# Sixteen attention heads of a fused attention and MLP kernel run ahead of the MLP, with 1024-column exponentials

## The chip, the cores and the metric

One core of a Trainium2 chip. The metric is the device time of one execution in microseconds (us), the median of the runs shown. Engines are named as in the profile: PE is TensorE, DVE is VectorE, ACT is ScalarE, POOL is GpSimd, SP is SyncE. Here POOL issues the loads from HBM, which cast fp32 to fp16; SP issues the stores, the small copies and the DMA transposes.

## What is computed

Causal attention with a forget gate, then a two-layer MLP on its output:

```python
scores = matmul(q, k.T) / sqrt(64)                  # q, k, v: (8 batches, 8 heads, 576, 64)
cum = cumsum(log(clip(f, 1e-4, 1)))                 # f: (8, 8, 576)
scores = where(causal, -1e9, scores + cum[:, None] - cum[None, :])
x = softmax(scores) @ v                             # reshaped to (4608, 512)
h = x @ w_in                                        # w_in: (512, 2048)
out = (h - tanh(h)) @ w_out                         # w_out: (2048, 512), out: (4608, 512) fp32
```

## The kernel before

Attention goes by *pairs* of heads of one batch, 32 pairs, each in one *slot*. The scores of a pair are held transposed (keys on partitions) in seven tiles (`TILES`, L264): three of 512 columns per head, and tile 3 (`LAST`) of 128 columns that holds the last key block of both heads. `scores` (L274) does one tile: matmuls over 67 rows (64 of the head and three rows that add the decay `cum`, which SP copies into `QT` and `KT`, L168 to L180) into one of two PSUM banks, then one exponential on ACT into an fp16 tile `e`. In the first four slots (`early`) the causal mask is added by a further matmul (L295), for the first pair's tiles 0 and 1 the decay also comes by matmuls (`direct`, L289); in all later slots POOL masks `e` with an affine_select (L311). `values` (L314) multiplies the exponentials with V and normalises on DVE into `xn`; `turn` (L338) brings `xn` into the ring `XR` of MLP inputs, for batch 0 by transposes on PE and a copy, later by two DMA transposes on SP.

Q and K of batches 0 and 1 are loaded by `load_qk` (L84), turned on PE by `trans` (L242) and copied into `QT` and `KT` by DVE, with every second column of the target written by one copy. Q and K of batches 2 to 7 are loaded in blocks of 128 rows (`load_block`, L89), turned by five DMA transposes each on SP (`turn_block`, L94) and put in place by four DVE copies each (`place`, L98). `LOADS` (L198, L212 to L225) says at which tile of which slot each of these is emitted. `spin` (L237) is matmuls of no use to the result.

The MLP goes by *units* of 512 tokens, nine in all. A first-layer step (`mlp1`, L369) is four matmuls of 512 columns, a tanh on ACT and an add on DVE; there are 16 per unit. The second layer of unit 0 is 16 plain steps (`mlp2`, L438); of the other units it is 14 half products (`product`, L394) of eight 256-column matmuls each, a seven-product scheme with sums of activations on DVE (`sums`, L383) and with sums of the weights (`wsum`, L233), which are made once, in slots 7 to 10. A store to the output (`settle`, L423) goes out on SP.

The order on every engine is the order of emission. Slots 0 to 4 have lists by hand (`BEGIN`, `ORDER`, `THEN`, L454 to L456); into slot 4 three MLP steps are mixed, into slots 5 to 32 seven or eight each (L520), evenly among the score tiles. What is left, 62 steps, runs at the end alone.

Of the kernel before, what the change touches and what calls it, by code (L numbers as in the profile page):

```python
# [22 lines left out]
def kernel(  # L23
# [31 lines left out]
    aex = ctx.enter_context(tc.tile_pool(name="aex", bufs=10))  # L55
# [72 lines left out]
    pick_k = WS[3].rearrange("p k e -> p (k e)")[:, 0:512]  # L128
    pick_q = cst.tile([P, P], FP16)
# [4 lines left out]
    EL = [cst.tile([P, 192], FP16, tag=f"el{i}", name=f"el{i}") for i in range(3)]  # L134
    nc.vector.memset(id16, 0.0)
# [5 lines left out]
    nc.vector.memset(minus16, -1.0)  # L141
    nc.vector.memset(neg16, 0.0)
    nc.vector.memset(tri16, 0.0)
    nc.gpsimd.affine_select(out=neg16, in_=neg16, compare_op=ALU.not_equal,
# [3 lines left out]
    for i in range(2):  # L148
        nc.vector.memset(KT[i][:, :, S:PITCH], 0.0)
    nc.vector.memset(pick_k, 0.0)  # L150
    nc.vector.memset(pick_q, 0.0)
    nc.vector.memset(cqs[NH:P, :], 0.0)
    nc.vector.tensor_scalar(out=lf, in0=lf, scalar1=0.0001, scalar2=1.0,
                            op0=ALU.max, op1=ALU.min)
    nc.scalar.activation(out=lf, in_=lf, func=AF.Ln)
    nc.vector.memset(pick_k[0:1, :], -1.0)
    nc.vector.memset(pick_q[0:1, :], 1.0)
# [5 lines left out]
    nc.scalar.activation(out=cq, in_=cum, func=AF.Copy, bias=-SHIFT * inv_qscale, scale=inv_qscale)  # L163
    nc.vector.scalar_tensor_tensor(out=clo, in0=cum, scalar=inv_qscale, in1=chi,
                                   op0=ALU.mult, op1=ALU.subtract)
    nc.vector.memset(pick_k[NH:NH + 1, :], -1.0)

    def load_aug(b):  # L168
        i, h0 = b % 2, b * H
        nc.sync.dma_start(out=KT[i][D:D + 1, :, 0:S], in_=chi[h0:h0 + H, :])  # L170
        nc.sync.dma_start(out=QT[i][D + 2:D + 3, :, :], in_=cq[h0:h0 + H, :])
        nc.sync.dma_start(out=KT[i][D + 1:D + 2, :, 0:S], in_=cc[NH + h0:NH + h0 + H, :])

    def const_rows(i):
        nc.sync.dma_start(out=QT[i][D:D + 2, :, :], in_=minus16)
        nc.sync.dma_start(out=KT[i][D + 2:D + 3, :, 0:S], in_=ones16[0:H, :])

    const_rows(0)
    load_aug(0)
    const_rows(1)  # L180
    load_qk(qn, q, 0, 4, H)
    load_qk(kn, k, 0, 4, H)
    for e in EL:
        nc.gpsimd.memset(e, 0.0)
    for i in range(2):
        nc.gpsimd.memset(vn[i][D:P, NJ - 1, :, :], 0.0)
        nc.gpsimd.memset(vn[i][:, :, :, D:VW], 1.0)
    load_v(0)
# [5 lines left out]
    def load_wout(t0, t1):  # L194
# [3 lines left out]
    LOADS = {(0, 0): [lambda: load_qk(qn, q, 1, 0, 2), lambda: load_qk(kn, k, 1, 0, 2),  # L198
                      lambda: load_win(0, DFF // 2)],
             (0, 3): [lambda: load_qk(qn, q, 1, 2, H), lambda: load_qk(kn, k, 1, 2, H)],  # L200
             (1, 0): [lambda: load_v(1)],
             (1, 3): [lambda: load_win(DFF // 2, DFF)],
             (2, 0): [lambda: load_wout(0, NFT // 2)],
             (3, 0): [lambda: load_wout(NFT // 2, NFT)]}
# [4 lines left out]
    for n in range(4):  # L209
        for i in range(2):  # L210
            LOADS.setdefault((NPAIR + 3 + n, 1 + 3 * i), []).append(lambda n=n, i=i: wsum(n, i * K2 // 2, (i + 1) * K2 // 2))
    for b in range(2, B):  # L212
        p0 = (b - 1) * NPAIR
        q0, k0, v0, tq, tk = {2: (5, 10, 21, 14, 16), 3: (-2, 3, 9, 6, 12)}.get(b, (-7, 0, 7, 4, 11))
        for n in range(NJ):
            at_tile(p0, q0 + n, lambda b=b, n=n: load_block(qb, q, b, n))
            at_tile(p0, k0 + n, lambda b=b, n=n: load_block(kb, k, b, n))
            at_tile(p0, v0 + n, (lambda b=b, n=n: load_v_block(b, n, 0, H)) if n < NJ - 1 else lambda b=b: load_v_rest(b))
            at_tile(p0, tq, lambda b=b, n=n: turn_block(TQ, qb, b, n))
            at_tile(p0, tk, lambda b=b, n=n: turn_block(TK, kb, b, n))  # L220
        at_tile(p0, 0, lambda b=b: load_aug(b))
        for n, (dst, src) in enumerate(((QT, TQ), (KT, TK))):
            for a in range(2):
                for c in (0, 2):
                    at_tile(p0 + 3, 2 * n + a + (n + 1 if b == 2 else 0), lambda b=b, dst=dst, src=src, a=a, c=c: place(dst, src, b, a, c))  # L225
# [11 lines left out]
    def spin(n):  # L237
        t32 = ps_tr.tile([P, UW], FP32, tag="tr", name="spin")
        for _ in range(n):
            nc.tensor.matmul(out=t32, lhsT=ones16[:, 0:P], rhs=ones16[:, 0:UW])  # L240

    def trans(b, c, src, dst, early, eng, by_head=False):  # L242
        pn, g3 = S // NT6, NT6 // 2
        if early:
            t32 = ps_m.tile([P, UW], FP32, tag="m", name="t32")
        else:
            t32 = ps_tr.tile([P, UW], FP32, tag="tr", name="t32")
        t16 = t32.bitcast(FP16)[:, 0:2 * S // 2].rearrange("p (a g n) -> p a g n", a=2, g=g3)
        for a in range(2):
            for g in range(g3):  # L250
                nc.tensor.transpose(out=t16[:, a, g, :],  # L251
# [315 lines left out]
```

## Time and profile before

| | us |
|---|---|
| median of 3 runs | 357.75 (355.23 to 357.9) |
| the profiled execution | 358.62 |
| its span, first to last instruction | 356.9 |
| PE / DVE / ACT / POOL busy in the span | 339.8 / 257.4 / 218.8 / 165.3 |
| mean granted PE clock | 0.974 of full |

The page's second part cuts the span into 40 slices and shows busy tenths for each engine. The chain follows the work that ended last back to the start. A group line gives the source line, engine, operation, output and input tiles with shapes, the count, then busy time and mean ns of one, then idle time of the engine before them and what ended it. A "q" behind an engine's name (SPq) is its instruction queue, where DMAs are issued.

### The profile page before, as it was taken

Reading aid. Unit: us, or ns where it says so; the run is one execution under the profiler, and the core shown is the slowest. Engines: PE = TensorE matmul, PEld = TensorE weight load, DVE = VectorE, ACT = ScalarE, POOL = GpSimd, SP = SyncE. Lnnn points to the kernel's source line nnn. Section 1 sums busy time; section 2 is a strip of 40 time slices with the busy share of each in tenths; the row PEclk is TensorE's granted clock in tenths of the full one; section 3 lists DMA queues with packets and bytes.
Section 4 is the critical chain, followed back from the end, with each engine's and each line's share of the span. In section 5 each row is a group of like instructions: output and inputs, shape, how many; then the busy total and the mean of one; then the engine's idle time right before and its main releaser. Section 6 shows DMA issues by size and latency. Waiting matters only on the chain.

```text
span 356.9 us, 8463 instructions
## 1 busy us (share of the span) xinstructions
PE 339.8 (95%) x3192; PEld 229.8 (64%) x3192; DVE 257.4 (72%) x501; ACT 218.8 (61%) x416; POOL 165.3 (46%) x324
## 2 busy tenths in 40 slices
PE   6698799999999999999999999999999999899995
PEld 3366455555567756887887568756887786386474
DVE  8557489963899489938893899389838855864871
ACT  6468377557775587558755875587558734533630
POOL 8941157498757755775567557753222310000000
PEclk9769889999999999999999999999999999999999
DMA  7999999999999997999799989994221112002002
GB/s 106 160 203 188 208 103 112 131 181 166 152 117 109 159 172 83 102 150 175 94 107 148 189 84 93 159 184 59 55 94 28 26 50 90 2 29 91 0 17 103
DMA packets 157469, 39.98 MB, mean 112 GB/s; under 512 B 142276, under 2 KB 155828, under 8 KB 157428
## 3 DMA queue, kind: packets, MB, share of 16 engines
q0 software_dynamic: 100128, 18.36, 70.3%
q1 hardware_dynamic: 57300, 21.09, 33.5%
q8 instruction: 25, 0.41, 0.5%
q14 instruction: 16, 0.13, 0.1%
HBM read 36.85 MB, written 9.44 MB: 130 GB/s over the span
## 4 chain that ended last, share of the span: by engine, by line
PE 79%; DVE 10%; ACT 3%; DMA 3%; SPq 2%; issue 2%; DVEq 0%; ACTq 0%
PE hps L366 29%; PE px L413 15%; PE ps L287 12%; PE pm L413 12%; PE av L322 8%; DVE gt L379 4%; PE ops L444 2%; DVE sm L392 2%; DMA QT<-cqs 2%; ACT e L301 2%; ACT th L373 2%; SPq L96 1%; DMA TK<-kn 1%; PE t L251 1%; DVE xn L334 1%
## 5 line engine op out<-in xcount | busy, mean ns | idle before, releaser
L366 PE MATMUL hps<-XR,win 128*128 128x512 f16 (+4 forms) x704 | 143.7, 344 | 2.0 <-DVE gt L379 2.0
L301 ACT ACTIVATE e<-ps 128x512 f16<-128x512 f32 x192 | 110.9, 596 | 30.5 <-PE ps L287 19.4
L373 ACT ACTIVATE th<-hps 128x512 f32<-128x512 f32 x144 | 86.3, 599 | 53.4 <-PE hps L366 47.1
L379 DVE TENSOR_TENSOR gt<-hps,th 128x512 f16<-128x512 f32 x144 | 96.7, 686 | 23.7 <-ACT th L373 22.1
L311 POOL TENSOR_SCALAR_AFFINE_SELECT e<-e 128x128 f16<-128x128 f16 x168 | 62.4, 373 | 107.8 <-ACT e L301 107.4
L366 PEld LDWEIGHTS <-win 128*128 128x128 f16 x704 | 62.4, 98 | 53.4 <-issue 7.2
L287 PE MATMUL ps<-QT,KT 67*128 67x64 f16 (+5 forms) x384 | 77.8, 285 | 5.1 <-DMA QT<-cqs 2.7
L287 PEld LDWEIGHTS <-KT 67*128 67x128 f16 (+1 forms) x384 | 37.5, 100 | 28.8 <-issue 6.4
L413 PEld LDWEIGHTS <-gt 128*128 128x128 f16 x512 | 48.0, 97 | 10.2 <-DVE gt L379 1.3
L413 PEld LDWEIGHTS <-sm 128*128 128x128 f16 x384 | 36.1, 97 | 5.4
L322 PEld LDWEIGHTS <-e 128*128 128x128 f16 x896 | 33.0, 98 | 5.6 <-issue 1.7
L322 PE MATMUL av<-vn,e 128*128 128x65 f16 x896 | 34.8, 195 | 1.3 <-DVE xn L334 1.0
L434 DVE TENSOR_TENSOR ost<-pm,part 128x512 f32<-128x512 f32 x24 | 16.5, 686 | 22.7 <-PE pm L413 8.2
L428 ACT ACTIVATE part<-px 128x512 f32<-128x512 f32 x24 | 14.3, 597 | 30.1 <-PE px L413 30.1
L413 PE MATMUL pm<-ws,gt 128*128 128x256 f16 x256 | 32.2, 272 | 0.0
L413 PE MATMUL px<-ws,sm 128*128 128x256 f16 x256 | 31.5, 272 | 0.0
L110 POOL DMA_DIRECT2D vn<-in_v_dram x32 | 28.4, 889 | 2.5 <-issue 1.4
L332 DVE TENSOR_SCALAR rs<-av 128x10 f32<-128x10 f32 (+1 forms) x33 | 5.3, 160 | 32.2 <-PE av L322 32.2
L334 DVE TENSOR_TENSOR xn<-av,rs 128x640 f16<-128x640 f32 (+1 forms) x33 | 26.5, 804 | 1.3 <-DMA out_dram<-ost 0.2
L91 POOL DMA_DIRECT2D qn<-in_q_dram x30 | 25.9, 864 | 2.1 <-issue 1.8
L91 POOL DMA_DIRECT2D kn<-in_k_dram x30 | 25.5, 849 | 1.4 <-issue 1.2
L413 PE MATMUL pm<-wout,gt 128*128 128x256 f16 x128 | 17.2, 273 | 0.2 <-DVE gt L379 0.2
(74 smaller groups left out, 291.9 us busy)
## 6 DMA issues: line engine op xcount, KB each, us to landing
out_dram<-ost SPq DMA_DIRECT2D x36, 256.0 KB
vn<-in_v_dram POOLq DMA_DIRECT2D x32, 128.0 KB, 6.3
qn<-in_q_dram POOLq DMA_DIRECT2D x24, 128.0 KB, 4.0
kn<-in_k_dram POOLq DMA_DIRECT2D x24, 128.0 KB, 5.1
win<-in_moe_w_in_dram POOLq DMA_DIRECT2D x2, 1024.0 KB, 11.8
wout<-in_moe_w_out_dram POOLq DMA_DIRECT2D x2, 1024.0 KB, 17.1
XR<-xn SPq DMA_TRANSPOSE x56
vn<-in_v_dram POOLq DMA_DIRECT2D x8, 64.0 KB, 6.9
```

Source lines behind the costliest of these rows:

```text
L91: nc.gpsimd.dma_start(out=dst[b % 2][0:pn, n, :].rearrange("p (h d) -> p h d", h=H), in_=src[b, :, n * P:n * P + pn, :].rearrange("h p d - ...
L110: nc.gpsimd.dma_start(out=vn[b % 2][:, n, h0:h1, 0:D], in_=v[b, h0:h1, n * P:(n + 1) * P, :].rearrange("h p d -> p h d"))
L287: nc.tensor.matmul(out=ps[:, col:col + n], lhsT=KT[b % 2][0:rows, h, j * P:(j + 1) * P], rhs=QT[b % 2][0:rows, h, i0:i0 + n], start=True, ...
L301: nc.scalar.activation(out=e[:, lo:hi], in_=ps[:, lo:hi], func=AF.Exp, scale=qscale)
L311: nc.gpsimd.affine_select(out=view, in_=view, compare_op=ALU.is_ge, fill=0.0, base=0, pattern=pat, channel_multiplier=-1)
L322: nc.tensor.matmul(out=av[:, a, ib, :], lhsT=E.pop((b, c, a, j, ib)), rhs=vn[b % 2][:, j, 2 * c + a, 0:D + 1], start=(j == 0), stop=(j == ib))
L334: nc.vector.tensor_tensor(out=xn[:, :, h0 * D:(h0 + hn) * D].rearrange("p i (a d) -> p a i d", a=hn), in0=av[:, h0:h0 + hn, :, 0:D], in1=r ...
L366: nc.tensor.matmul(out=hps[:, o:o + n], lhsT=win[:, ci, ft * P:(ft + 1) * P], rhs=XR[:, ci, t:t + n], start=(ci == 0), stop=(ci == NCH - 1))
L373: nc.scalar.activation(out=th, in_=hps, func=AF.Tanh, scale=-1.0)
L379: nc.vector.tensor_tensor(out=GT[(u, ft)], in0=hps, in1=th, op=ALU.add)
L413: nc.tensor.matmul(out=ps[:, g * E2:(g + 1) * E2], lhsT=left(k), rhs=right[:, k, :], start=(first and g == 0 and k == 0), stop=(k == K2 - ...
L434: nc.vector.tensor_tensor(out=ost, in0=ps, in1=PART.pop((u, {2: 1, 7: 5, 4: 6}[n])), op=ALU.add)
```

## The change

- Batches 0 and 1 become eight slots with hand-written lists (`FIRST`); no MLP step is mixed into slots 0 to 6, and no spin follows slot 0. Slot 7 gets 4 steps. Slot 8 has no scores: it finishes pair 7, runs 30 MLP steps, and turns and places batch 2 between them. Then slots follow with 5 (pairs 8 to 11), 6 (pair 12), and 7 or 8 steps; 60 steps are left for the end.
- Slots 1 to 6 take score tiles in twos: two PSUM banks, one exponential of 1024 columns. The groups alternate between the two score banks (`SC`) and two of the three MLP banks (`MB`), which are idle then. The `e` tiles are twice as wide, 6 instead of 10.
- The causal mask is added by matmul in all of the first eight slots.
- `load_qk` puts rows in another order on the partitions: each row of 64 numbers is now a run of its own (128 bytes in SBUF, 768 before), and the copies after `trans` write runs of 96 columns.
- The first head gets its decay by matmuls in all its tiles (`direct`); its three rows in QT and KT are zero until slot 4. Memsets are reordered, some move from POOL to DVE and behind the first scores.
- `turn` uses PE for pair 3 alone; pairs 0 to 2 go by DMA transposes.
- Loads of batch 0, 1 and the weights are issued in one row on POOL, w_in in quarters; batch 2 follows them.
- Unit 0 takes the seven-product scheme too; the weight sums are made at steps 14, 16, 19 and 21. `mlp2` is gone.

The diff, cut to its core:

```diff
-    ps_sc = ctx.enter_context(tc.tile_pool(name="ps_sc", bufs=2, space=PSUM))
-    ps_m = ctx.enter_context(tc.tile_pool(name="ps_m", bufs=3, space=PSUM))
+    SC = ps_sc.tile([P, 2, UW], FP32, tag="sc", name="sc")
+    MB = ps_m.tile([P, 3, UW], FP32, tag="m", name="mb")
...
     def load_qk(dst, src, b, h0, h1):
-            out=dst[b % 2][:, h0:h1, :, :].rearrange("p h n d -> p h (n d)"),
-            in_=src[b, h0:h1, :, :].rearrange("h (p n) d -> p h (n d)", n=NT6))
+            out=dst[b % 2][:, h0:h1, :, :].rearrange("p h n d -> p (h n) d"),
+            in_=src[b, h0:h1, :, :].rearrange("h s d -> (h s) d").rearrange("(m p) d -> p m d", p=S // NT6))
...
-                to = dst[b % 2][0:D, h0:h0 + an, e:S:2].rearrange("d a (p g) -> d a p g", g=g3)
-                of = t16[e * D:(e + 1) * D, a0:a0 + an, :, :].rearrange("d a g p -> d a p g")
+                to = dst[b % 2][0:D, h0:h0 + an, 0:S].rearrange("d a (g e p) -> d a g e p", g=g3, e=2)[:, :, :, e, :]
+                of = t16[e * D:(e + 1) * D, a0:a0 + an, :, :]
...
+    PLACE = {0: (0, 0), 1: (0, 1), 2: (1, 0), 4: (1, 1), 5: (2, 0), 6: (2, 1)}
+    GROUPS = [(0, 1), (2, 4), (5, 6), (LAST,)]
...
+        if how == "group":
+            banks = bank("g", [SC, MB[:, 0:2, :]])
...
-        nc.scalar.activation(out=e[:, lo:hi], in_=ps[:, lo:hi], func=AF.Exp, scale=qscale)
+        nc.scalar.activation(out=eb[:, :, lo:hi], in_=banks[:, 0:n2, lo:hi], func=AF.Exp, scale=qscale)
...
+    for at, n in ((NFT - 2, 0), (NFT, 2), (NFT + 3, 1), (NFT + 5, 3)):
+        mlp[at] += [(wsum, n, 0, K2 // 2), (wsum, n, K2 // 2, K2)]
...
+    FIRST = [["8", "q0", "k0", "5", "q1", "4", "s0", "s1", "k1", "p", "s2", "s4", "s5", "q2", "r", "s6", "s3"],
+             ["g0", "g1", "k1", "g2", "va", "vb", "q2", "x", "g3"],
+             ["g0", "va", "g1", "k1", "vb", "g2", "q2", "x", "g3"],
+             ["g0", "va", "g1", "k1", "vb", "g2", "q2", "x", "g3"],
+             ["c", "g0", "va", "g1", "k1", "vb", "g2", "x", "q2", "g3"],
+             ["g0", "g1", "k1", "g2", "va", "vb", "x", "g3"],
+             ["g0", "va", "g1", "q1", "vb", "x", "g2", "k1", "g3"],
+             ["b", "s0", "va", "s1", "vb", "m", "s2", "x", "m", "s3", "s4", "m", "s5", "m", "s6"],
+             ["va", "m", "vb", "m", "x"] + ["m"] * 16 + ["tq"] + ["m"] * 4 + ["tk"] + ["m"] * 4 + ["pq"] + ["m"] * 4 + ["pk"]]
...
-            take = 0 if p < NPAIR else 3 if p == NPAIR else 7 if p <= 2 * NPAIR + 1 or p % 2 == 0 else 8
+            take = 5 if p < 3 * NPAIR else 6 if p == 3 * NPAIR else 8 - p % 2
```

In the lists, a number is that many spins, `q`/`k` a `trans` of the pair so many slots on, `s` a score tile, `g` a group of two (g3 is tile 3), `va`/`vb` the values of the slot before by head, `x` its `turn`, `m` an MLP step, `b` the loads of batch 2, `tq`/`tk` its DMA transposes, `pq`/`pk` its placement, `c` the first head's rows and batch 2's decay rows, `p` and `r` memsets (and batch 1's rows).

More of the change, by code (lines that the diff above doesn't have):

```diff
@@ L312, in scores, with values @@
                                 base=0, pattern=pat, channel_multiplier=-1)
-    def values(b, c, heads=(0, 1), apart=False):
-        if 0 in heads:
+    def values(b, c, a):
+        if a == 0:
             av = ps_av.tile([P, 2, 512], FP32, tag="av", name="av")
@@ new lines, in att_items @@
+    def att_items(p):
+        items = []
+        before = pairs[p - 1]
+        for ti in range(len(TILES)):
+            if p < len(pairs):
+                items.append((lambda ti=ti: scores(*pairs[p], (ti,), "late"), True))
+            items += [(load, False) for load in LOADS.get((p, ti), ())]
+            if ti == 1 and p > 2 * NPAIR:
+                items += [(lambda a=a: values(*before, a), a == 1) for a in range(2)]
+                items.append((lambda: turn(*before), True))
+        return items
@@ L524 @@
             for emit, counts in items:
+                emit()
                 n += counts
-                if emit is None:
-                    first = n
-            whole, n = n, 0
-            for emit, counts in items:
-                if emit is not None:
-                    emit()
-                n += counts
-                while n > first and (given + 1) * (whole - first) <= (n - first) * len(mine):
-                    fn, *args = mine[given]
-                    fn(*args)
+                while given < take and (given + 1) * whole <= n * take and STEPS[0] < len(mlp):
+                    step()
@@ L536 @@
                     given += 1
-        for fn, *args in mlp[at:]:
-            fn(*args)
+        while STEPS[0] < len(mlp):
+            step()
 _INS = ['q', 'k', 'v', 'f', 'moe_w_in', 'moe_w_out']
```

393 lines of the change are left out of this document (200 added, 193 removed).

## The prediction

> **What bounds the kernel now.** I read the page first (engines, slices, chain), then stretches of the span, the chain in order of time, and the groups by shape.
>
> ```profile
> span 356.9 us, 8463 instructions
> PE 339.8 (95%) x3192; PEld 229.8 (64%) x3192; DVE 257.4 (72%) x501; ACT 218.8 (61%) x416; POOL 165.3 (46%) x324
> ...
> PEclk9769889999999999999999999999999999999999
> ...
> PE 79%; DVE 10%; ACT 3%; DMA 3%; SPq 2%; issue 2%; DVEq 0%; ACTq 0%
> ```
>
> TensorE bounds it: busy for 95% of the span and 79% of the chain. The granted clock is below nine tenths only among the first six slices of 8.9 us, and it is these that the change rebuilds. So the question is how soon a common state is reached: both kernels have emitted 60 MLP steps (3+7+7+7+7+7+7+8+7 before, 4+30+5+5+5+5+6 after) and the scores of 13 pairs at the end of slot 12. After that only the count of steps left differs, 212 before and 210 after.
>
> ```profile
> 28.20:33.15 4.95, 4.58 (x74) 3.41 (x72) 4.35 (x8) 4.11 (x9) 0.87 (x1) 1.00 1.87 182
> 27.45:30.87 3.42, 3.04 (x38) 2.04 (x36) 3.31 (x6) 2.81 (x7) 1.35 (x2) 1.00 2.28 161
> 34.28:37.70 3.42, 1.88 (x35) 1.30 (x32) 1.62 (x4) 2.25 (x5) 0.29 (x1) 1.00 1.17 207
> 37.70:41.10 3.40, 3.40 (x19) 1.60 (x16) 0.85 (x3) 1.19 (x2) 0.69 (x2) 0.50 1.24 210
> 74.50:118.40 43.90, 43.34 (x401) 27.32 (x402) 33.47 (x66) 28.87 (x57) 33.15 (x60) 1.00 1.69 142
> 297.80:313.10 15.30, 14.28 (x66) 6.28 (x65) 12.71 (x22) 8.96 (x15) 0.00 (x0) 1.00 0.09 31
> ```
>
> Columns: stretch, its length, busy time of PE, PEld, DVE, ACT, POOL, granted clock, DMA share, GB/s. An early slot (first row) lasts 4.95 us with no engine full. Slots 8 to 12 of before are the fifth row: 43.9 us, PE 99% busy, ending at 118.4. The last row is the first layer of one MLP unit with nothing beside it: sixteen steps in 15.3 us, 0.96 each. A stretch in which PE was busy 1.88 of 3.42 us was followed by one at clock 0.50; one with 3.04 of 3.42 was not.
>
> **The change, part by part**, as a sum of stages up to the end of slot 12.
>
> *Slot 0.* Before, the second pair's scores began at 18.36:
>
> ```profile
> 8.06 5.92 DMA QT<-cqs
> ...
> 18.36 0.59 PE ps L287
> ...
> 116.80 0.88 PE px L413 x8
> ```
>
> The small row copies into QT/KT took 5.92 us to land and PE stood until they had. After, fewer memsets stand before the scan (an estimate of 0.5 us), the scale copy of cum goes between head 0's copies, and head 0's third tile needs no copied rows: one score tile (about 0.9 us at half clock) leaves the far side of the stall, and four banks drop the waits on ACT there. I take 16.3 for the start of slot 1 (bounds 15 and 18.4). The stall itself stays, and with it the half clock.
>
> *Slots 1 to 6.* The prices are those of the first 47 us, by shape:
>
> ```profile
> L301 ACT ACTIVATE e<-ps 128x512 f16<-128x512 f32 x30 | 17.6, 600 | 12.5 <-PE ps L295 8.1 <-PE ps L287 3.1 <-PE ps L292 0.8
> ...
> L262 DVE COPY QT<-t 64x576 f16<-64x576 f16 x10 | 8.0, 800 | 4.7 <-PE t L251 4.5
> ...
> L301 ACT ACTIVATE el<-ps 128x128 f16<-128x128 f32 x5 | 1.4, 274 | 2.2 <-PE ps L287 2.1 <-PE ps L295 0.2
> ...
> L348 DVE COPY XR<-x 128x576 f16<-128x576 f16 x1 | 0.5, 458 | 2.6 <-PE x L346 2.6
> ```
>
> An exponential of 512 columns takes 0.600 us, of 128 columns 0.274: 0.85 ns a column, so 1024 columns take about 1.03 us; the other bound is two of today's, 1.20. I take 1.03, as both rows lie on one line. ACT per slot: 3x1.03+0.27 = 3.4 us (before 3.9, and 0.6 for XR). The Q and K copies no longer write with a stride: 0.46 (the unstrided copy of the last row, same size) to 0.80 us each, four per pair, so DVE needs between 4.35-4x0.34 = 3.0 and 4.35 us a slot (4.35 by the early slot's row). PE streams 3200 score, 1152 mask, 1950 value and 1152 transpose columns; at 8x256 columns in 0.88 us (the row at 116.80) that is 3.2 us. Three engines near 3.3 us, but banks tie them: group 2 reuses the two banks of group 0, and the next slot's group 0 waits until ACT has read group 2. By the same column rate PE comes to the end of group 2 after 0.56+0.45+0.61+0.28+0.45+0.63 = 2.98 us (scores 0, values, scores 1, transposes, values, scores 2), ACT starts some 0.2 later and takes 1.03: 4.3 us a slot. Bounds: 3.6 (ACT alone with its gaps) and 6.9 (all at half clock: 6.4 us of PE and half a wait). I take one slot at half clock and the rest at 4.3: 6x4.3+2.6 = 28.4, so slot 7 starts at 44.7. The masks of batch 1 now cost PE 4x0.49 us and POOL nothing; both are inside this. The XR transposes moved to SP: two issues of about 1.3 us a slot (the price of the SP rows below), hidden under 4.3.
>
> *Loads.* The Q and K loads of batches 0 and 1 become runs of 128 bytes instead of 768. Packets and MB in one us from 8 (768-byte rows of Q and K), in one us from 13 (128-byte rows of V), and in two us from 18 (weights):
>
> ```profile
> q0 software_dynamic: 171, 0.13, 104.6%
> ...
> q0 software_dynamic: 1151, 0.15, 251.0%
> ...
> q0 software_dynamic: 227, 0.40, 113.2%
> ```
>
> The short packets move 0.15 MB/us against 0.13, so they cost nothing here. 3.54 MB of batches 0 and 1 take 25 us from about 3, w_in 2.1 MB at 0.20 another 10.5 to 39, w_out to 49, and with seven pairs of XR transposes among them perhaps 56; step 0 needs w_in at about 46, step 16 w_out at about 63. Hidden. The Trainium skill, page "DMA: Bandwidth & Descriptors", Specifications, says that transfers below 512 B fall to read-modify-write and lose line rate. By it the change would pay on each of these loads; the two rows above show the opposite order at these sizes, so the sum leaves it out.
>
> *Slot 7* adds four MLP steps to a pair with masks on PE: 1.8+0.9+4x0.88 = 6.2 us, to 50.9.
>
> *Slot 8: MLP alone.* Two value halves and two steps 2.6 us, ten first-layer steps at 0.96, six products at 0.88: 17.5 us. VectorE also gets the weight sums, which before lay in slots 7 to 10:
>
> ```profile
> L235 DVE TENSOR_TENSOR ws<-wout x4: 682/692/760, 66.2 to 78.1; 128x1024 f16<-128x1024 f16 x4
> ```
>
> Two of them (1.4 us) stand ahead of the last first-layer add, two more ahead of the third product's operand, on an engine (DVE) that was busy 12.71 of 15.3 us in the last row above: I take 2 us (bounds 0 and 2.8). Step 21 ends at 70.4.
>
> *Batch 2's Q and K turn on SP, the decisive part.* Before, the chain ran through exactly this:
>
> ```profile
> 65.16 1.22 SPq L96
> ...
> 70.42 3.23 DMA TK<-kn
> ...
> 73.86 0.56 DVE KT L99
> ```
>
> and a store to the output takes SP's queue 0.53:
>
> ```profile
> 88.16 0.53 SPq L450 DMA_DIRECT2D out_dram<-ost  x1
> ```
>
> Five transposes in a row start 5.26 us apart, first to last: 1.31 each; the last lands 3.23 us after its start. After, SP's order is: the store of product 2 (step 21), five TQ, the store of product 7, five TK. SP starts when step 21's sum is added (0.9 us after it, an estimate: one add of 512 columns and the wait for it): 0.53+5x1.31+0.53+4x1.31+3.23+0.56 = 16.6 us, so the first score tile of batch 2 can start at 87.9. PE has twelve steps to do meanwhile (22 to 33, 10.6 us). And VectorE stands at the Q placement until TQ has landed, with the adds of steps 30 to 33 queued behind it, so that PE stops after three of them (three MLP banks) and again before the scores: some 7 us of idle PE, enough by the row at 34.28 for the clock to fall again.
>
> *Slots 8 to 12* then: 26 steps of 0.88 (22.9 us), five pairs' scores of 1.4, four pairs' values of 0.85 (each by its columns) = 33.3 us on PE; plus 0.9 for waits (before lost 0.56 of 43.9 us, and PE was ahead of POOL there), 1.7 for one 3.4 us window at half clock, and POOL:
>
> ```profile
> L311 POOL TENSOR_SCALAR_AFFINE_SELECT e<-e 128x128 f16<-128x128 f16 x168 | 62.4, 373 | 107.8 <-ACT e L301 107.4
> ...
> L91 POOL DMA_DIRECT2D kn<-in_k_dram x30 | 25.5, 849 | 1.4 <-issue 1.2
> ```
>
> Slot 8 has seven masks and seven loads on POOL, 2.6+6.1 = 8.7 us, while PE needs 6.6; the values of that pair wait for its masks: 2.4 us over two slots (0 if POOL keeps up). Sum 38.3, so slot 12 ends at 126.2 instead of 118.4: +7.8.
>
> *The rest.* Two steps fewer: unit 0 takes fourteen products of eight 256-column matmuls (0.88) instead of sixteen steps of four 512-column ones (the same 2048 columns): -1.7.
>
> **Sum**: +7.8-1.7 = +6.1 on the profiled execution's 358.62 us (span 356.9 and 1.7 around it), 364.7. That execution lies 0.9 above the median of 357.75, so I predict **363.8 us**, its own range 359 to 369.
>
> **Rivals.**
> 1. *The attention slots do not hold the clock.* The spin matmuls that filled the early slots are gone (only slot 0 has some); 3.2 of 4.3 us is 74%, between the 55% busy that lost the clock and the 89% that kept it. If every second window falls, a slot takes about 5.6: 6x1.3-2.6 = +5, 369; if it never rises, 6x2.6-2.6 = +13, 377. The Trainium skill, "TensorE: Matmul & The Clock Gate", Part 1, lets the clock fall after an idle window of about 3.4 us; no slot has such a gap, so by it 363.8 stands. The row at 34.28 is stricter: it was more than half busy.
> 2. *Not slower: the turn of batch 2 is hidden.* If K is placed when PE comes to it, 7.1 us of idle PE and 1.7 of clock go: 354.9. It decides where nine spaces between starts and the 4.85 us around them fit into the 9.7 us that PE has left, at 0.54 us per transpose, against 1.31 in the rows above; for it speaks only that the DMA queues are empty then, while the 3.23 us of landing was measured among loads. Partly so (a landing of 2 us, no POOL wait) gives 360.
> 3. *Short packets are slow.* At half the rate of Q and K's loads, 2.36 MB take 18 us more, w_out comes at about 74 instead of 63: step 16 waits some 10 us, 374. The two packet rows speak against it. (It is what the Trainium skill's "DMA: Bandwidth & Descriptors", Specifications, would lead to.)
> 4. *The wide exponential gains nothing* (1.20 us): slots of 4.5, +1: 365, not to be told from the forecast.
>
> **How the numbers follow.** Forecast with rival 4: 0.52 (0.40 slower than before by over 1%, 0.12 within 1%); rival 1: 0.15 (slower); rival 2 and its partial form: 0.27 (0.16 faster, 0.11 within); rival 3: 0.06 (slower). One per cent is about what a measurement of this kernel can tell from no change. So slower 0.61, same 0.23, faster 0.16. The range 352 to 371 leaves out the worst of rivals 1 and 3 and the best of rival 2.
>
> **What would show it.** Each step has a mark in the profile after: slot 1 starting near 16; exponentials of 1024 columns near 1.03 us; slots of 4.3 us at clock 1.00; copies into QT below 0.8 us; SP's transposes on the chain between 71 and 88, VectorE's place waiting for TQ and TK, PE idle some 7 us there; POOL ending waits in slots 8 and 9; slot 12 ending near 126. The prediction is wrong if PE is busy through 75 to 88, or if the slots run below 4 us.

## The result, and the profile after

The changed kernel takes **659.81 us** (median of 4 runs, 656.01 to 664.63) where the kernel before takes 356.56 (4 runs, 355.23 to 357.9): 1.851 times as long, 95% interval 1.834 to 1.868. Here and below a ratio compares fast runs only, which leaves out three of the seven runs of E8 (365.62 to 366.92) and one of the twelve of E12 (361.29). The forecast was 363.8 with a range to 371. It and all four rivals were wrong by hundreds of microseconds, so something is at work that none of them names.

The page of the changed kernel, its profiled execution of 664.63 us:

```profile
span 662.9 us, 8560 instructions
PE 470.7 (71%) x3266; PEld 278.6 (42%) x3266; DVE 258.2 (39%) x523; ACT 223.9 (34%) x395; POOL 161.4 (24%) x300
...
PEclk9668757756798759975976598659975965586559
```

DVE, ACT and POOL are as busy as before (258.2 against 257.4 us, 223.9 against 218.8, 161.4 against 165.3). PE has 131 us more busy time for about the same matmuls (the clock line says why: it is below full almost to the end, not in six slices) and stands idle for 662.9-470.7 = 192 us, against 17 before. What ends this idle time is in the view of waits (waiting line, what it waited for, us in total, times, longest):

```profile
ACT th L410 <- PE mb L407: 291.1, 144, 7.3
DVE gt L416 <- ACT th L410: 286.6, 140, 3.1
...
PE mb L407 <- DVE gt L416: 129.3, 105, 1.6
...
PE sc L337 <- ACT e L353: 34.7, 43, 1.0
```

The first-layer matmuls wait 105 times for the add, the add 140 times for the tanh, the tanh 144 times for the matmuls. Each waits for the other, in a ring. The kernel before had 2.0 us of waits of these matmuls for the add. The timeline, with the MLP alone (start, length, engine and instruction, in brackets the idle time before it and what ended it):

```profile
84.52 0.69 DVE L416 TENSOR_TENSOR gt<-mb,th 128x512 f16<-128x512 f32 x1 [1.67 <-ACT th L410]
85.26 1.86 PE L407 MATMUL mb<-XR,win 128*128 128x512 f16 x4 [1.41 <-DVE gt L416]
87.16 0.60 ACT L410 ACTIVATE th<-mb 128x512 f32<-128x512 f32 x1 [2.68 <-PE mb L407]
87.79 0.69 DVE L416 TENSOR_TENSOR gt<-mb,th 128x512 f16<-128x512 f32 x1 [2.58 <-ACT th L410]
88.54 1.87 PE L407 MATMUL mb<-XR,win 128*128 128x512 f16 x4 [1.41 <-DVE gt L416]
```

Four matmuls, then the tanh, then the add, then the next four matmuls: one step every 3.28 us, nothing beside anything. The same stage of the kernel before:

```profile
298.71 5.13 PE L366 MATMUL hps<-XR,win 128*128 128x512 f16 x23
298.75 0.60 ACT L373 ACTIVATE th<-hps 128x512 f32<-128x512 f32 x1 [2.07 <-PE hps L366]
299.38 0.69 DVE L379 TENSOR_TENSOR gt<-hps,th 128x512 f16<-128x512 f32 x1 [0.86 <-ACT th L373]
299.62 0.60 ACT L373 ACTIVATE th<-hps 128x512 f32<-128x512 f32 x1 [0.27 <-PE hps L366]
```

There 23 matmuls, nearly six steps, run without a gap, and the tanhs and adds of earlier steps lie beside them. The windows view of the changed kernel (length, busy PE, PEld, DVE, ACT, POOL, granted clock, DMA share, GB/s) shows what follows from the gaps:

```profile
80.00:90.00 10.00, 5.76 (x14) 1.76 (x13) 2.93 (x5) 1.79 (x3) 0.00 (x0) 0.50 0.00 0
```

The clock is at half: four matmuls take 1.86 us instead of 0.86 to 1.02.

**Theory 1 (T1).** The change makes the three MLP banks one tile, `MB [P, 3, UW]`, and the two score banks one tile, `SC [P, 2, UW]`. The waits are placed per tile, not per bank: a matmul into bank 1 of `MB` waits for the readers of bank 0. The rivals: **T2**, the clock is lost in the slots without spins and the waits only follow from it; **T3**, the order itself (eight attention slots, then the MLP alone) is what costs.

### The profile page after: what moved, and what is told of

It is laid out like the page before. It is cut to its first block, busy times and chain, and to the rows that moved or that the text cites. A ratio compares the mean times of both kernels' runs of the same rounds, so it can differ in the third digit from the quotient of the medians.

```text
span 662.9 us, 8560 instructions
## 1 busy us (share of the span) xinstructions
PE 470.7 (71%) x3266; PEld 278.6 (42%) x3266; DVE 258.2 (39%) x523; ACT 223.9 (34%) x395; POOL 161.4 (24%) x300
## 3 DMA queue, kind: packets, MB, share of 16 engines
q0 software_dynamic: 116640, 18.36, 41.0%
## 4 chain that ended last, share of the span: by engine, by line
PE 59%; ACT 17%; DVE 15%; issue 4%; DMA 2%; SPq 2%; POOL 1%; DVEq 0%; ACTq 0%; POOLq 0%
PE mb L407 33%; DVE gt L416 12%; ACT th L410 11%; PE px L447 8%; PE mb L447 5%; ACT e L353 5%; PE sc L337 5%; PE av L374 4%; DMA out_dram<-ost 2%; PE mb L337 1%; SPq L107 1%; POOL e L364 1%; DVE sm L429 1%; DVE ost L468 1%; DVE xn L382 1%
## 5 line engine op out<-in xcount | busy, mean ns | idle before, releaser
L407 PE MATMUL mb<-XR,win 128*128 128x512 f16 (+4 forms) x704 | 226.4, 472 | 136.5 <-DVE gt L416 129.3
L416 DVE TENSOR_TENSOR gt<-mb,th 128x512 f16<-128x512 f32 x144 | 99.5, 691 | 286.6 <-ACT th L410 286.6
L407 PEld LDWEIGHTS <-win 128*128 128x128 f16 x704 | 82.6, 123 | 253.2 <-issue 235.2
L410 ACT ACTIVATE th<-mb 128x512 f32<-128x512 f32 x144 | 86.0, 597 | 291.1 <-PE mb L407 291.1
L353 ACT ACTIVATE e<-sc 128x512 f16<-128x512 f32 (+1 forms) x166 | 103.8, 625 | 59.8 <-PE sc L337 42.9
L337 PE MATMUL sc<-QT,KT 67*128 67x192 f16 (+4 forms) x349 | 90.1, 330 | 39.5 <-ACT e L353 34.7
L337 PEld LDWEIGHTS <-KT 67*128 67x128 f16 x384 | 42.1, 113 | 79.1 <-issue 65.6
L447 PE MATMUL mb<-ws,gt 128*128 128x256 f16 x288 | 36.0, 272 | 0.0
L382 DVE TENSOR_TENSOR xn<-av,rs 128x640 f16<-128x640 f32 x32 | 26.4, 825 | 1.1
L447 PE MATMUL px<-wout,gt 128*128 128x256 f16 x144 | 22.1, 318 | 0.0
```

What stands on the lines that cost most here:

```text
L337: nc.tensor.matmul(out=ps[:, col:col + n], lhsT=KT[b % 2][0:D + 3, h, j * P:(j + 1) * P], rhs=QT[b % 2][0:D + 3, h, i0:i0 + n], start=True ...
L353: nc.scalar.activation(out=eb[:, :, lo:hi], in_=banks[:, 0:n2, lo:hi], func=AF.Exp, scale=qscale)
L382: nc.vector.tensor_tensor(out=xn.rearrange("p i (a d) -> p a i d", a=2), in0=av[:, :, :, 0:D], in1=rs.to_broadcast([P, 2, NJ, D]), op=ALU. ...
L407: nc.tensor.matmul(out=hps[:, o:o + n], lhsT=win[:, ci, ft * P:(ft + 1) * P], rhs=XR[:, ci, t:t + n], start=(ci == 0), stop=(ci == NCH - 1))
L410: nc.scalar.activation(out=th, in_=hps, func=AF.Tanh, scale=-1.0)
L416: nc.vector.tensor_tensor(out=GT[(u, ft)], in0=hps, in1=th, op=ALU.add)
```

## The experiments

**E1: five tiles of one bank.** The order, the loads and everything else as in the changed kernel; the groups of two become single tiles with exponentials of 512 columns.

```diff
-    SC = ps_sc.tile([P, 2, UW], FP32, tag="sc", name="sc")
-    MB = ps_m.tile([P, 3, UW], FP32, tag="m", name="mb")
+    SC = [ps_sc.tile([P, 1, UW], FP32, tag=f"sc{i}", name=f"sc{i}") for i in range(2)]
+    MB = [ps_m.tile([P, 1, UW], FP32, tag=f"m{i}", name=f"mb{i}") for i in range(3)]
```

> Edit: the changed kernel with its five banks as five PSUM tiles of one bank each (two for scores, three for the MLP) instead of one tile of two and one of three; the groups of two become single score tiles with exponentials of 512 columns that cycle over four banks. Order of work, loads and everything else as in the changed kernel. T1 (a matmul into one bank of a tile waits for the readers of the other banks of the same tile, so that the first-layer step becomes matmul, tanh, add in series): the 105 waits of PE for the add's result (129.3 us) and the granted clock of 0.50 in the MLP-alone stretch go; a first-layer step alone is back at about 0.96 us; the whole takes 360 to 378 us at a mean clock above 0.94. T2 (the clock is lost by the eight attention slots without spins and never comes back; the waits only follow from it): stays above 550 us, clock below 0.80. T3 (the order itself, eight slots ahead and the MLP alone behind them, is what costs): stays above 500 us with the idle time of PE in slot 8 and after.

Measured: 370.2 us (369.95 to 370.45), 1.039 times before (1.034 to 1.044). Its page:

```profile
span 368.5 us, 8558 instructions
PE 338.2 (92%) x3266; PEld 234.0 (64%) x3266; DVE 255.2 (69%) x523; ACT 216.9 (59%) x413; POOL 163.8 (44%) x300
...
PEclk9999899985999999999999999999999999999999
...
L411 PE MATMUL mb<-XR,win 128*128 128x512 f16 (+4 forms) x704 | 146.2, 347 | 12.2 <-DVE gt L420 5.3
```

The 129.3 us of waits are 5.3, the clock is full but for two dips. T1 gave this number; T2 and T3 gave over 500. Of the 294 us between the two spans, 132.5 are busy time of PE (470.7 against 338.2: the clock) and 162 its idle time (192.2 against 30.3: the waits).

**E2: the exponentials of 1024 columns kept, the MLP's banks apart.** In slots 0 to 6 two tiles of two banks and one of one; from slot 7 on five tiles of one bank. This is the change as I had read it.

```diff
+    SC = ps_e.tile([P, 2, UW], FP32, tag="sc", name="sc")
+    MB = ps_e.tile([P, 2, UW], FP32, tag="m", name="mb")
+    TB = ps_e.tile([P, UW], FP32, tag="t", name="tb")
...
+        if p == 7:
+            split_banks()
```

> Edit: the changed kernel with the exponentials of 1024 columns kept. In slots 0 to 6 the banks are two tiles of two banks and one of one; from slot 7 on they are five tiles of one bank. T1: slots 1 to 6 as in the changed kernel (slot 7 starts at about 59 us), no serial first-layer steps behind it, so 372 to 390 us: the forecast of 363.8 plus what the two-bank tiles cost in the slots (slot 7 at 59 instead of 44.7), less what is gained where the slots' PE has more time. Against the kernel with single tiles everywhere the difference is then the price of the exponential of 1024 columns over one tile: T1 says that this one is the slower by 3 to 12 us, my forecast (1.03 instead of 1.20 us per two tiles) says that it is the faster by 1 to 5 us. T2 and T3 as for the first kernel: above 500 us.

Measured: 373.87 us (371.51 to 375.45), 1.049 times before (1.042 to 1.055), as T1 says; and 3.7 slower than E1, as T1 says too, where the forecast had the wide exponential as a small gain. Slot 7 starts at 47.65 us and not at the 59 that I expected from the changed kernel, where the turning of Q and K shares the tile of three banks; here it has a tile of its own (this was not tested by itself). Two rows of E2's timeline:

```profile
12.52 0.35 PE L346 MATMUL sc<-QT,KT 67*128 67x448 f16 x1 [0.69 <-ACT e L362]
...
33.01 0.38 PE L346 MATMUL sc<-QT,KT 67*128 67x512 f16 x1 [0.79 <-ACT e L362]
```

In slot 0 the second score tile goes to the other bank of `SC` and yet waits for the first one's exponential. That and its like put the start of slot 1 at 17.90 us (E1: 14.02), and slot 1 then ran at half clock: 6.20 us at 0.50, against 4.47 in E1 at 1.00. In the later slots a group cannot start until the whole exponential of its two banks is done, 1024 ns by its row among the groups by shape:

```profile
L362 ACT ACTIVATE e<-sc 128x1024 f16<-128x1024 f32 x12 | 12.3, 1024 | 5.6 <-PE sc L346 3.7 <-PE sc L354 1.8
```

In slots 2 to 6 PE waits 1.9 us for exponentials in E2 and not at all in E1, and these five slots take 23.55 us against 22.98. So of the 6.2 us by which E2 starts slot 7 later, 3.9 come from slot 0, 1.7 from the half clock in slot 1, and only 0.6 from the slots behind it.

**E3: the waits filled.** The changed kernel with six matmuls of no use behind the four of each first-layer step.

```diff
+        fill = ps_tr.tile([P, UW], FP32, tag="tr", name="fill")
+        for _ in range(6):
+            nc.tensor.matmul(out=fill, lhsT=ones16[:, 0:P], rhs=ones16[:, 0:UW])
```

> Edit: the changed kernel, with six matmuls of 512 columns of no use to the result (1.28 us at full clock) behind the four of each first-layer step, so that PE does not stand while it waits for the add. It parts the loss into the waits and the clock. T1: the step stays serial (matmuls, tanh 0.60, add 0.69, some 0.06 between them), but at clock 1.00: 2.3 to 2.5 us a step instead of 3.28; 144 of them with the other 216 us of PE work make 540 to 590 us at a clock above 0.90, so some 100 of the 300 us were the clock's and 200 the waits'. T2 (the clock is the root and the waits follow from it): with the clock held the adds run ahead again, tanh and add lie beside the matmuls of the next steps as in the kernel before, and the step is what PE does in it, 0.86+1.28 = 2.14 us or less. T3: no change of the waits, the time longer by the added matmuls, above 700 us.

Measured: 612.93 us (one run), mean clock 0.98. Its timeline in the stretch with the MLP alone:

```profile
90.44 1.02 PE L407 MATMUL mb<-XR,win 128*128 128x512 f16 x4
...
91.30 1.46 PE L411 MATMUL fill<-ones 128*128 128x512 f16 x6
91.50 0.60 ACT L413 ACTIVATE th<-mb 128x512 f32<-128x512 f32 x1 [1.84 <-PE mb L407]
92.13 0.69 DVE L419 TENSOR_TENSOR gt<-mb,th 128x512 f16<-128x512 f32 x1 [1.74 <-ACT th L413]
...
92.87 1.02 PE L407 MATMUL mb<-XR,win 128*128 128x512 f16 x4
```

With the clock at full the step is still a ring, 92.87-90.44 = 2.43 us, inside T1's 2.3 to 2.5 and over T2's 2.14: the clock is not the root. The changed kernel agrees where its own clock is still 1.00: four matmuls start at 70.57 and the next four at 73.00 (PE's timeline, shown with the clock below). So with the MLP alone 0.85 of the 3.28 us is the clock's, and the rest of the way down to 0.96 is the waits'.

My total for T1 (540 to 590) was too low: 144 steps of 2.43 make 350 us, and the other work then took 263, not 216; among it are 32.8 us in which score matmuls waited for exponentials. The total does not part the loss cleanly. The added matmuls fill the waits of the steps (first-layer matmuls wait 0.3 us in all for the add, instead of 129.3), but they are 212 us of PE work, and where a step did not have to wait they cost time themselves. So the 243 us by which the span is longer than E1's are an upper bound for what remains of the 294 with the clock held; at least some 50 were the clock's.

**E4: the kernel before with its three MLP banks as one tile**, nothing else.

```diff
-    ps_m = ctx.enter_context(tc.tile_pool(name="ps_m", bufs=3, space=PSUM))
+    ps_m = ctx.enter_context(tc.tile_pool(name="ps_m", bufs=1, space=PSUM))
+    MB = ps_m.tile([P, 3, UW], FP32, tag="m", name="mb")
```

> Edit: the kernel before, with its three MLP banks as one PSUM tile of three banks instead of three tiles of one; nothing else. T1: the same serial first-layer steps, a hundred or so waits of PE for the add of 1 us and more each, and a clock that falls: 500 to 660 us, without any of the change's reordering. T2 (spins and slots) and T3 (order): within 1% of the kernel before, since its order and its spins are untouched.

Measured: 636.44 us (one run). Its page and its waits:

```profile
PE 468.0 (74%) x3192; PEld 272.8 (43%) x3192; DVE 262.1 (41%) x501; ACT 221.1 (35%) x416; POOL 161.8 (25%) x324
...
PEclk7896679865975698568857895789577855595559
```

```profile
PE mb L373 <- DVE gt L386: 137.6, 120, 2.0
```

With the old order and the old spins, this edit alone reproduces the loss: the same ring, the same clock. E1 and E4 together show T1 from both sides; T2 and T3 fall. What is left is the forecast itself: it gave +6.1 us for the change as read, and that change (E2) costs +17. The next runs go into its terms.

**E5: three store buffers instead of two**, on E1 (and two instead of three for the partial sums, to make room). In E1 the turn of batch 2's Q and K looks as forecast:

```profile
69.76 0.43 SPq L473 DMA_DIRECT2D out_dram<-ost  x1
70.30 7.97 SPq L107 DMA_TRANSPOSE TQ<-qn  x5
...
78.37 0.54 SPq L473 DMA_DIRECT2D out_dram<-ost  x1
79.00 6.43 SPq L107 DMA_TRANSPOSE TK<-kn  x5
80.95 0.69 DVE L472 TENSOR_TENSOR ost<-mb,part 128x512 f32<-128x512 f32 x1 [8.01 <-DMA out_dram<-ost]
...
81.69 1.87 PE L411 MATMUL mb<-XR,win 128*128 128x512 f16 x4 [4.33 <-DVE ost L472]
...
88.55 1.03 PE L341 MATMUL sc<-QT,KT 67*128 67x512 f16 x3 [2.70 <-DVE KT L110]
```

but DVE stands at the add of product 4, whose buffer is free only when product 7's store has landed; and that store is queued on SP behind the five transposes.

> Edit: the kernel with single-bank tiles (370.2 us), with three buffers for the sums that go to the output instead of two (and two instead of three for the partial sums). In it, the add of product 4's sum on DVE waited 8.01 us for a store that SP issued only behind the five transposes of Q, and the first-layer adds stood behind it, so that PE idled 4.3 us. Theory A (my forecast's wording: the placement of Q, which needs the transposes to have landed, is what DVE stands at; the store only hides it): the wait moves to the placement of Q, and the time falls by 0 to 1.5 us. Theory B (the store's buffer alone is the cause): the 4.3 us of idle PE and a part of the clock go, 4 to 6 us faster.

Measured: 365.15 us (363.76 to 367.89), 1.024 times before (1.018 to 1.030), 5 us less than E1. That is theory B's number, but not its mechanism: PE still waits twice, 2.94 and 3.19 us where E1 had 4.33 and 2.70:

```profile
81.86 1.87 PE L412 MATMUL mb<-XR,win 128*128 128x512 f16 x4 [2.94 <-DVE gt L421]
86.92 1.03 PE L342 MATMUL sc<-QT,KT 67*128 67x512 f16 x3 [3.19 <-DVE KT L111]
```

The wait has moved to the placement of Q, as theory A says: DVE now stands 2.36 us there for the transposes. From the sum of step 21 to batch 2's first score it is 16.5 us instead of 18.8. Of the 4.0 us between the two profiled spans that is 2.3; another 1.6 is a wait of a first-layer step for an output turned by DMA (`XR`), 2.2 us in E1 and 0.6 in E5, which neither theory names and which was not followed up. So both were there: the store's buffer, and behind it the placement of Q, which takes over part of the wait.

**E6: more MLP steps to cover the turn**, on E5: 38 in slot 8, three a slot in slots 8 to 11.

```diff
-["tq"] + ["m"] * 4 + ["tk"] + ["m"] * 4 + ["pq"] + ["m"] * 4 + ["pk"]]
+["tq"] + ["m"] * 4 + ["tk"] + ["m"] * 8 + ["pq"] + ["m"] * 8 + ["pk"]]
...
-            take = 5 if p < 3 * NPAIR else 6 if p == 3 * NPAIR else 8 - p % 2
+            take = 3 if p < 3 * NPAIR else 6 if p == 3 * NPAIR else 8 - p % 2
```

> Edit: as the kernel with three store buffers, and 38 instead of 30 MLP steps in slot 8 (twelve between the transposes of Q and their placement, twenty to that of K), three instead of five in slots 8 to 11. Forecast step tested: the chain on SP for batch 2's Q and K leaves PE some 7 us idle and one window at half clock. T1 with that step right: the idle time at 80 to 90 us and the half clock go, 7 to 9 us; but slots 8 to 11 have then 4.9 us of PE work each against 24 us of POOL work in the four (28 masks of 0.37 and 15 loads of 0.9), so 3 to 6 us come back as waits for POOL: 362 to 368 us. If SP's chain costs nothing that other work does not cost too: 370 us and more.

**E9: E6 with the masks of slots 8 to 11 on PE.**

```diff
-                items.append((lambda ti=ti: scores(*pairs[p], (ti,), "late"), True))
+                items.append((lambda ti=ti: scores(*pairs[p], (ti,), "late" if p >= 3 * NPAIR else "two"), True))
```

> Edit: as the kernel with 38 steps in slot 8, and in slots 8 to 11 the causal mask is added by a matmul of the identity with one tile of large negative numbers instead of by POOL (the first eight slots use the same tile). If POOL is what slots 8 to 11 wait for (my forecast's term of 2.4 us, made larger by three steps a slot): 3 to 6 us less than the kernel with POOL's masks, 358 to 363 us. If POOL's share is hidden there: 2 us more than it, for the 28 mask matmuls on PE.

Measured: E6 372.86 us (370.83 to 374.35), E9 373.28 (371.75 to 374.15): both 8 us slower than E5. E6 has the number of its second case, though that case's reason (the chain on SP costs nothing of its own) does not hold, as the turn became shorter; E9 is outside both of its cases. Rows of E6 (windows over slots 8 to 11) and of E9 (windows over the same slots, then its timeline):

```profile
92.00:129.00 37.00, 30.69 (x314) 21.61 (x313) 19.18 (x40) 22.67 (x45) 33.89 (x62) 0.95 2.12 138
```

```profile
98.00:131.00 33.00, 31.39 (x353) 23.85 (x354) 17.23 (x40) 21.97 (x44) 6.00 (x12) 0.95 0.86 93
```

```profile
79.68 9.37 SPq L108 DMA_TRANSPOSE TK<-kn  x5
...
86.63 1.98 DVE L111 COPY QT<-TQ 64x1152 f16<-64x1152 f16 x4 [3.67 <-DMA TQ<-qn]
...
89.38 5.87 PE L408 MATMUL mb<-XR,win 128*128 128x512 f16 x20 [6.11 <-DVE gt L417]
```

In E6 batch 2's first score starts at 91.87 with eight more steps done (E5: 86.92), a gain of some 2 us at 0.88 a step; then POOL is busy 33.9 of 37 us and PE idles 6.3 (by name only 1.6 of it for POOL), and a first-layer step behind these slots waits 3.4 us for `XR`. Pair 12's outputs come at 133.80, in E5 at 128.02. In E9 POOL no longer binds these slots (6.0 of 33 us; PE idles 1.6). But with no masks in its queue that have to wait for scores, it issues batch 3's loads from 70 us on, while batch 2's transposes run: DVE stands 3.67 us at the placement of Q until they land, K's take 9.37 us to issue instead of 6.44 in E6, PE waits 6.11, and the first score comes at 97.95. A cover was taken away twice: the steps that hid POOL, then the masks that held the loads back.

**E8: the new row order of Q and K alone**, on the kernel before.

```diff
-            in_=src[b, h0:h1, :, :].rearrange("h (p n) d -> p h (n d)", n=NT6))
+            in_=src[b, h0:h1, :, :].rearrange("h s d -> (h s) d").rearrange("(m p) d -> p m d", p=S // NT6))
```

> Edit: the kernel before with one part of the change alone: rows of Q and K of batches 0 and 1 in the new order (runs of 128 bytes in SBUF instead of 768) and the copies behind their transposes writing runs of 96 columns. My forecast (short packets cost nothing, the copies fall from 0.80 to 0.46 us): same to 2 us faster, 354 to 356 us, copies at 0.46, loads landing as before. Rival 3 of the forecast (short packets at half the rate): weights land 10 us or more later and the first MLP steps wait, 358 to 366 us.

Measured: 360.39 us (7 runs, 357.82 to 366.92) against 357.22, 1.0066 times (1.002 to 1.011). The copies fell to 0.45 us as expected, and the kernel became no faster; a little slower, if anything. Rival 3's 10 us are not there. By what way the 2 us come was not separated.

**E7: unit 0 by seven products alone**, on the kernel before (weight sums at steps 16, 18, 21 and 24).

```diff
-    mlp = [(fn, 0, s) for fn in (mlp1, mlp2) for s in range(NFT)]
+    mlp = []
...
-    for u in range(1, NU):
+    for u in range(NU):
```

> Edit: the kernel before with one part of the change alone: unit 0 takes the seven-product scheme, the weight sums are made at steps 16, 18, 21 and 24 instead of in slots 7 to 10, the sixteen plain steps of unit 0 are gone. My forecast's step (two MLP steps fewer at the end, 2048 columns less on PE): 1.7 us faster. The other case: the weight sums (8 x 0.69 us on DVE) and the sums of activations come while DVE is at 93 to 97% of its time (50 to 70 us), and DVE makes PE wait: same or up to 3 us slower.

Measured: 366.3 us (364.56 to 367.26), 1.028 times before (1.022 to 1.035): 10 us slower, more than either case. Its waits and a window:

```profile
PE px L410 <- DVE ws L232: 3.2, 1, 3.2
```

```profile
60.00:70.00 10.00, 7.17 (x75) 4.61 (x71) 9.75 (x20) 4.97 (x11) 4.25 (x9) 1.00 0.96 114
```

DVE is busy 9.75 of 10 us and PE 7.17, where before DVE had 9.66 and PE 9.99. PE's own work fell as forecast (338.5 against 339.8 us); the sums went to the engine that was full. From 60 to 80 us PE idles 5.3 us (before 0.3), half of the loss; where the rest lies was not followed.

**E10: four banks in the early slots**, on the kernel before: its score tiles of slots 0 to 3 over four single-bank tiles, head 0's decay by matmuls in all its tiles, no spins after slot 0, outputs of pairs 0 to 2 turned by DMA. **E11** is E10 and E7 together. **E12** is E10 with the old spins and the old turning on PE.

```diff
+        turns_of[0] += 1
+        if early and turns_of[0] % 4 > 1:
+            ps = ps_m.tile([P, 512], FP32, tag="m", name="pt")
...
-            direct = (b, c) == (0, 0) and ti < 2
+            direct = (b, c, a) == (0, 0, 0)
```

> Edit: the kernel before with the score tiles of its first four slots going over four banks (each a tile of its own) instead of two, head 0's decay by matmuls in all of its tiles, no spins after slot 0, and the outputs of pairs 0 to 2 turned by DMA; the MLP begins in slot 4 as before, and nothing of the order after it changes. If what the kernel with single-bank tiles gained up to the start of slot 1 (14.0 instead of 18.4 us) and in slots 1 to 3 (3.4 to 3.8 instead of 4.95 us) can be kept with the old order behind it: slot 4 starts 4 to 7 us earlier and the whole is 3 to 7 us faster, 350 to 354 us. If the loads of w_in and of batch 1 set the pace there, the gain is given back as waits for them: 355 to 358 us.

> Edit: the two preceding edits together. If both terms hold and add up: 5 to 8 us faster than before, 349 to 352 us. If the seven-product scheme in unit 0 meets a full DVE, it is slower than the kernel with four banks alone by up to 3 us.

> Edit: the kernel before with only two things of the change: the score tiles of its first four slots go over four banks, each a tile of its own, and head 0's decay comes by matmuls in all of its tiles (with four spins more in slot 0). Spins in slots 1 to 3 and the turning of outputs on PE stay as before, unlike in the kernel with four banks run earlier, which lost the clock to 0.50 from 20 to 40 us and then waited 4.2 us for a DMA-turned output. If these two are what ate the gain: slot 1 starts near 15.5 instead of 18.4 us, the clock stays near 1.00 through slots 1 to 3 and the whole is 2 to 4 us faster than before, 352 to 354 us. If the pace up to the MLP's start is set elsewhere (the loads of batch 1 and w_in, or ACT), slot 4 starts when it did and the time is within 1 us of before.

Measured: E10 362.94 us (361.55 to 364.81), 1.020 times before (1.013 to 1.026); E11 370.77 (370.07 to 374.46), 1.044 (1.034 to 1.053); E12 355.45 (12 runs, 354.56 to 361.29) against 356.36, 0.9986 times (0.9954 to 1.0018). E10's window and wait, and E12's clock:

```profile
20.00:30.00 10.00, 9.79 (x97) 7.52 (x95) 7.60 (x12) 6.25 (x13) 2.75 (x4) 0.50 1.50 180
```

```profile
PE hps L373 <- DMA XR<-xn: 4.2, 1, 4.2
```

```profile
PEclk9989999999999999999999999999999999999999
```

In E10 the clock falls to half and stays there from 20 to 40 us (a slot takes 6.6 us), and the first MLP step waits 4.2 us for a DMA-turned output. With spins and PE's turning back (E12) the clock is held and slot 4 starts at 33.12 instead of 35.52, but of these 2.4 us the times show nothing beyond their uncertainty. No version here beats the kernel before for certain; E12 is level with it.

## Why the prediction was wrong

**The step that failed** is this sentence of slots 1 to 6: "banks tie them: group 2 reuses the two banks of group 0, and the next slot's group 0 waits until ACT has read group 2", and with it "ten first-layer steps at 0.96", taken from a row of a kernel whose banks are three tiles. It assumes that what ties work together is the bank. It is the tile (E1, E4). The price is not a term that was mis-sized but one that is missing: 3.28 us a step instead of 0.96 with the MLP alone, some 290 us in all. The diff showed it: `ps_m` with `bufs=3` became one tile with a dimension of three. No row of before could show the wait, since no tile there had two banks in use by different engines; the bound for an unseen wait should have been "matmul + tanh + add in series", 0.86+0.60+0.69 = 2.15 us, against 0.96.

The Trainium skill, page "Perfetto Trace Analysis", Optimizing Tensor Performance (Matmuls), says that independent groups of matmuls should rotate through different PSUM banks, so that ACT and DVE empty one while the next fills. The changed kernel does rotate, and the overlap was gone all the same (105 waits, 129.3 us): the rotation has to be over tiles that the program keeps apart.

**The clock.** That the clock can fall without a long gap was right. But the forecast's reading, that a stretch with PE busy little over half loses it, does not hold throughout: the changed kernel kept 1.00 with 1.82 of 3.40 us. It lost the clock where the MLP stands alone, four matmuls of 1.02 us in 2.43, and then stayed at half:

```profile
67.00:70.40 3.40, 1.82 (x24) 1.20 (x23) 1.26 (x2) 1.93 (x4) 0.00 (x0) 1.00 3.01 140
73.80:77.20 3.40, 1.99 (x6) 0.55 (x4) 1.02 (x2) 0.60 (x1) 0.00 (x0) 0.70 0.19 43
77.20:80.60 3.40, 1.96 (x5) 0.55 (x4) 0.69 (x1) 0.60 (x1) 0.00 (x0) 0.50 0.00 0
```

```profile
70.57 1.02 PE L407 MATMUL mb<-XR,win 128*128 128x512 f16 x4 [0.62 <-DVE gt L416]
...
73.00 1.02 PE L407 MATMUL mb<-XR,win 128*128 128x512 f16 x4 [0.96 <-DVE gt L416]
75.44 1.86 PE L407 MATMUL mb<-XR,win 128*128 128x512 f16 x4 [1.41 <-DVE gt L416]
```

The rule quoted from the Trainium skill, page "TensorE: Matmul & The Clock Gate", Part 1 (an idle window of about 3.4 us) did not cover it, as the gaps are 1.41 us. Another paragraph of that Part 1 of the Trainium skill's page, on PE idling briefly between matmul groups that cycle through PSUM, says that the clock then goes up and down; the trace agrees that short gaps suffice, but here, with the MLP alone, it sits at half.

**The other terms**, measured where the missing one is absent (E2 is the change as read; times from the timelines; the forecast's 0.9 us from step 21 to its sum is in the third row; in the fifth its 38.3 us to the end of slot 12 with the 3.1 that pair 12's outputs came behind that end before):

| step of the forecast | forecast | E2 | E1 |
|---|---|---|---|
| start of slot 1 | 16.3 | 17.90 | 14.02 |
| slots 1 to 6 | 28.4 | 29.75 | 27.45 |
| slot 7 to the sum of step 21 | 26.6 | 28.2 | 28.3 |
| from there to batch 2's first score | 16.6 | 18.3 | 18.8 |
| from there to pair 12's outputs | 41.4 | 43.0 | 43.1 |
| idle PE in that turn | 7 | 6.5 | 7.0 |
| difference to before at pair 12's outputs | +7.8 | +15.7 | +10.1 |
| "the rest" | -1.7 | +1.1 | +1.5 |
| sum (spans) | +6.1 | +16.8 | +11.6 |

- *Slot 0*: the four banks are worth more than I took (14.02) when they are four tiles, and next to nothing when they are two (17.90, before 18.36).
- *Slots 1 to 6*: right in size, one slot at half clock (6.20 us in E2, 6.9 taken) and the rest at 4.7 instead of 4.3, in which there is a wait for K ahead of slot 7 (1.70 us in E2, 2.76 in E1) that I had not seen. The exponential of 1024 columns took 1.024 us (forecast 1.03), the copies 0.45 (bound 0.46). So rival 4's 1.20 us are not there; but the wide exponential gained nothing all the same, since PE waited 1.9 us for it over its two-bank tile.
- *Slots 7 and 8*: 1.6 us short in E2, 1.7 in E1. Behind the wait for K the clock fell, which the forecast had not put here: it is 0.94 over this row in both, and four first-layer matmuls at 43.22 us in E1 took 1.90 us. The waits for the weight sums were 1.10 us, under the 2 I took.
- *Batch 2's turn on SP*: right in place, in PE's idle time and in the fall of the clock, and some 2 us short, so rival 2 falls. Its own sum was a little off: 17.5 less 10.6 leaves 6.9 us of idle PE, not 7.1. The five transposes of Q took 7.97 us in E1, where 5x1.31 = 6.55 were taken. One link was wrong: DVE stood first at a store's buffer, only then at the placement of Q (E5).
- *Slots 8 to 12*: 1.6 us short. POOL's waits are small with five steps a slot (0.5 us in E1, 2.4 taken), and real with three (E6). In their place a first-layer step waited 2.2 us (1.9 in E2) for `XR`, which I had not priced.
- *The rest*: PE has less work, as forecast, but from 122 us on its first-layer steps wait longer for DVE: 4.4 us in E1 (the row below, from the waits of that stretch) and in E2, 2.0 before. Why they do was not separated. On the old order the scheme costs 10 us (E7), and there much of it where DVE is full, at 60 to 80 us. The term was counted on PE alone, while part of its work goes to DVE.

```profile
PE mb L411 <- DVE gt L420: 4.4, 11, 0.5
```

- *Rival 1* is real in another kernel: E10's slots are its "all at half clock" (6.6 us; 6.9 forecast). In E1, without spins as well, the clock held in slots 1 to 6. What decides between them stays open.
- *Rival 3*: no sign of 10 us (E8), and in E1's list of waits no matmul waits for w_out.

## What to carry to other kernels

When a change joins buffers into one tile, write down for every write into a part which reads of the other parts it will now wait for; bound that wait by the whole chain in series, even if the trace of before has no such row. Banks that different engines use at the same time belong in tiles of their own, and an instruction over two banks is bought with their independence. In a full kernel, count a step on the engine that receives its work, and before covering one wait with work from elsewhere ask what that work was covering there.

## What was not expected of the hardware

- Gaps of 1.41 us between bursts of 1.86 us keep the granted clock at 0.50 (every window from 77.2 to 97.6 us in the changed kernel); and E10 shows the other side: with PE busy 9.79 of 10 us, stretched by the half clock itself, it stayed at 0.50 for some 20 us. In slot 1 of E2, with PE busy 6.20 of 6.20 us at 0.50, it was back at 1.00 in the next slot.
- The five DMA transposes of K on SP took 6.43 us to issue in E1 (Q's 7.97) and 9.37 in E9, where loads were issued at the same time.
- A strided fp16 copy from PSUM of 64x576 took 0.80 us with every second column written and 0.45 with runs of 96.
